# The last batch of an attention and top-k MLP kernel chosen by ranking candidates above a floor, and score columns moved ahead of TensorE's transposes

## The chip, the cores and the metric

The kernel runs on one core of a Trainium2 chip. The metric is the device time of one execution in microseconds. Engines are named as in the profile: PE is TensorE (PEld its weight loads), DVE VectorE, ACT ScalarE, POOL GpSimd, and SP the engine whose queue issues most DMAs.

## The reference, cut to what matters

```python
# q: (4, 12288, 128)   kv: (4, 384, 32, 128)   w_sr: (128, 128)
kv_flat = pool_4x4_mean(kv).reshape(B, 768, 128) @ w_sr
k = v = kv_flat
s = (q @ k.transpose(0, 2, 1)) / sqrt(128)
a = exp(s - s.max(-1)); a /= a.sum(-1) + 1e-9
x = a @ v                                        # (4, 12288, 128)
scores = x @ w_gate                              # (4, 12288)
out = x.copy()
for b in range(4):
    top = argpartition(-scores[b], 128)[:128]    # capacity 128
    ye = relu(x[b, top] @ w1) @ w2               # 128 -> 1024 -> 128
    out[b, top] = x[b, top] + sigmoid(scores[b, top])[:, None] * ye
```

Each batch has 12,288 queries against 768 pooled keys. Of the 12,288 results the 128 with the highest gate score go through a two-layer MLP, and its gated result is added to their rows.

## The kernel before

The queries go in 192 blocks of 256 (48 a batch), each as two halves of 128 (`QT = 2`). A block's scores are a 128 x 1536 tile in PSUM: columns 0 to 767 for the first half, 768 to 1535 for the second. There are two such tiles, `s_buf[0]` and `s_buf[1]`, each three banks wide, and blocks take them in turn. A third tile, `o_two`, of two banks, takes the results of the attention matmuls.

`S(n, parts)` issues the scores of block n in four parts: 0 is columns 0 to 511, 1 is 512 to 767, 2 is 768 to 1023, 3 is 1024 to 1535. Each part is three matmuls, because queries and keys are split into a high piece (`qh`, `kh`) and low pieces (`ql`, `kl`, `kb`). `s_max` takes the row maxima on DVE (`m`), `exp` the exponentials on ACT (`am`), again in parts. In batches 0 to 2 (`by_pe`) PE transposes columns 1280 to 1535 of the exponentials (`turn_pe`), and DMA transposes the rest; in batch 3 DMA transposes all of them. `to_high` casts to 16 bits on ACT, `to_low` takes the remainder on DVE (the last 256 columns) or on POOL (the first 1280), and `turn` issues the DMA transposes on SP's queue (`at`). `AV` multiplies with the values, `LAG = 4` blocks later: 36 matmuls a block. `sums`, `recip` and `finish` normalise on DVE and store through SP. The gate score of each query is one more column of the values; POOL copies it into `scores` for every second block.

The main loop (lines 627 to 681) writes each engine's order out by hand: every engine runs its instructions in the order of the text (`InOrder`). Around the change it reads

```python
        if more:
            S(i + 1, (3,), bank0 + bank1)
        exp(i, 2 if by_pe(i) else 1)
        if by_pe(i):
            turn_pe(i)
        exp(i, 1 if by_pe(i) else 2)
        if more:
            S(i + 1, (2, 1), bank0)
            S(i + 1, (0,))
        to_high(i, 1)
```

Other work is fed in between by generators that stop at named points (`at_point`): the keys of the next batch (`next_keys`), and the top-k and expert of the batch before (`topk`, `pick`, in the list `select`).

After the loop four blocks n-3 to n are still without their attention matmuls (`out`, `norm`, `put`), and batch 2's expert is half done. Block n-3 goes to `o_two`, the other three each to a bank of `s_buf[0]` (`spare`); batch 2's expert writes bank 1 of `o_two`. Then comes the search of batch 3: the scores' bits become sortable 16-bit halves, and `find` determines the 128th largest bit by bit, two bits a step, in eight steps for the high half and eight for the low one. A step is three counting comparisons on DVE, a matmul with ones that sums them over the partitions, and three or four small instructions. Batch 2's remaining pieces advance by one at each step. `pick` turns the mask into the rows' indices with small matmuls against a triangle of ones, gathers the 128 rows by indirect DMA on POOL's queue, while 36 `warm` matmuls keep PE busy, runs the two layers and scatters the result back.

Of the kernel before, what the change touches and what calls it, by code (L numbers as in the profile page):

```python
# [19 lines left out]
P = 128  # L20
# [8 lines left out]
QT = 2  # L29
# [37 lines left out]
def attention_topk_mlp(ctx, tc, a, outs, capacity):  # L67
# [284 lines left out]
    def by_pe(n):  # L352
        return blocks[n][0] < B - 1
# [273 lines left out]
    for i in range(nb):  # L627
# [29 lines left out]
        if more:  # L657
            S(i + 1, (3,), bank0 + bank1)
        exp(i, 2 if by_pe(i) else 1)
# [3 lines left out]
        if more:  # L663
            S(i + 1, (2, 1), bank0)
            S(i + 1, (0,))
# [23 lines left out]
    def out(m):  # L689
        for j in range(QT):  # L690
            AV(m, j, dest[m])
# [15 lines left out]
    key = tk.tile([P, NCOL], I32, name="key")  # L707
    high, low, eqh, rest = (tk.tile([P, NCOL], U16, name=x) for x in ("high", "low", "eqh", "rest16"))
    junk = tk.tile([P, 3, NCOL], BF16, name="junk16")
    jt = tk.tile([P, 3], F32, name="jt")  # L710
    for j in range(3):
        pool.memset(jt[:, j:j + 1], float(j + 1))

    for m in (n - 3, n - 2):
        out(m)
        norm(m)
        put(m)
    out(n - 1)
    out(n)
    key_part(0, NCOL - 2 * QT)  # L720
# [5 lines left out]
    key_part(NCOL - 2 * QT, NCOL)  # L726
    dve.tensor_copy(low, key.bitcast(U16).rearrange("p (n h) -> p n h", h=2)[:, :, 0])

    counts = s_buf[1][:, 0, 0:4]

    def find(x, need, name):
        tv = tk.tile([P, 3], F32, name="tv")
        lo = tk.tile([P, 1], F32, name=name)
        dve.memset(lo, 0.0)
        dve.tensor_scalar(out=tv, in0=jt, scalar1=float(1 << 14), scalar2=None, op0=ALU.mult)
        for sh in range(14, -1, -2):
            cnt = tk.tile([P, 3], BF16, name="cnt3")
            for j in range(3):
                dve.tensor_scalar(out=junk[:, j], in0=x, scalar1=tv[:, j:j + 1], scalar2=None, op0=ALU.is_ge, op1=ALU.add, accum_out=cnt[:, j:j + 1])
            pe.matmul(counts[:, 0:3], ones16, cnt, start=True, stop=True)  # L740
            advance(select)
            if sh:
                base3 = tk.tile([P, 3], F32, name="base3")
                dve.tensor_scalar(out=base3, in0=jt, scalar1=float(1 << (sh - 2)), scalar2=lo, op0=ALU.mult, op1=ALU.add)
            dig = tk.tile([P, 1], F32, name="dig")
            hit = tk.tile([P, 3], F32, name="hit")
            dve.tensor_scalar(out=hit, in0=counts[:, 0:3], scalar1=need, scalar2=None, op0=ALU.is_ge, op1=ALU.add, accum_out=dig)
            if sh:
                tv = tk.tile([P, 3], F32, name="tv")
                dve.scalar_tensor_tensor(out=tv, in0=dig.broadcast_to([P, 3]), scalar=float(1 << sh), in1=base3, op0=ALU.mult, op1=ALU.add)  # L750
            dve.scalar_tensor_tensor(out=lo, in0=dig, scalar=float(1 << sh), in1=lo, op0=ALU.mult, op1=ALU.add)
        return lo

    th = find(high, float(capacity), "th2")
    gth = tk.tile([P, NCOL], BF16, name="gth")
    above = tk.tile([P, 1], BF16, name="above")
    dve.tensor_scalar(out=gth, in0=high, scalar1=th, scalar2=None, op0=ALU.is_gt, op1=ALU.add, accum_out=above)
    dve.tensor_scalar(out=eqh, in0=high, scalar1=th, scalar2=None, op0=ALU.is_equal)
    pe.matmul(counts[:, 3:4], ones16, above, start=True, stop=True)
# [7 lines left out]
    while select:  # L767
        advance(select)
    for _ in pick(b, mask):
        pass  # L770
# [31 lines left out]
```

## Time and profile before

| | us |
|---|---|
| runs | 978.61, 980.33, 980.29 |
| median | 980.29 |
| profiled execution: its time | 976.78 |
| its span, first to last instruction | 975.0 |
| PE busy in the span | 895.4 |
| DVE, ACT, POOL busy | 707.3, 756.1, 749.5 |

The profile is of one execution; times within it are counted from its first instruction. A row of the timeline has the start, the duration, the engine, the operation and what it writes and reads, and in brackets how long the engine stood idle ahead of it and what ended that. Matmuls are pipelined and their ends are modelled, so rows of one engine can overlap.

### The profile page before, as it was taken

Reading aid. Unit: us, or ns where it says so; the run is one execution under the profiler, and the core shown is the slowest. Engines: PE = TensorE matmul, PEld = TensorE weight load, DVE = VectorE, ACT = ScalarE, POOL = GpSimd, SP = SyncE. Lnnn points to the kernel's source line nnn. Section 1 sums busy time; section 2 is a strip of 40 time slices with the busy share of each in tenths; the row PEclk is TensorE's granted clock in tenths of the full one; section 3 lists DMA queues with packets and bytes.
Section 4 is the critical chain, followed back from the end, with each engine's and each line's share of the span. In section 5 each row is a group of like instructions: output and inputs, shape, how many; then the busy total and the mean of one; then the engine's idle time right before and its main releaser. Section 6 shows DMA issues by size and latency. Waiting matters only on the chain.

```text
span 975.0 us, 25800 instructions
## 1 busy us (share of the span) xinstructions
PE 895.4 (92%) x9886; PEld 727.3 (75%) x10067; DVE 707.3 (73%) x1732; ACT 756.1 (78%) x1177; POOL 749.5 (77%) x573
## 2 busy tenths in 40 slices
PE   3889999999999999999999999999999998999844
PEld 2668788777778787787788877787788876887743
DVE  6456666666777777777767777787868876888674
ACT  2668888888888887887888888888798987998700
POOL 1478898887788988888789898988778877688600
PEclk9999999999999999999999999999999999999966
DMA  9799999999999999999999999999999999999910
GB/s 357 207 225 200 246 237 212 219 250 232 223 188 232 232 237 233 228 223 233 212 195 231 234 226 241 221 185 221 180 194 232 240 226 235 253 217 234 224 48 6
DMA packets 600508, 211.31 MB, mean 217 GB/s; under 512 B 532288, under 2 KB 582592, under 8 KB 599616
## 3 DMA queue, kind: packets, MB, share of 16 engines
q1 hardware_dynamic: 600128, 209.12, 104.8%
q8 instruction: 79, 1.29, 0.6%
q0 software_dynamic: 256, 0.52, 0.2%
q14 instruction: 45, 0.37, 0.1%
HBM read 52.04 MB, written 25.43 MB: 79 GB/s over the span
## 4 chain that ended last, share of the span: by engine, by line
PE 62%; DMA 8%; ACT 7%; DVE 7%; issue 6%; POOL 3%; SPq 1%; POOLq 0%; ACTq 0%; DVEq 0%
PE s L52 33%; PE o_two L52 29%; DMA at<-hl 8%; ACT am L52 4%; DVE m L52 3%; ACT hl L52 2%; DVE junk L52 1%; POOL hl L52 1%; POOL ql L52 1%; POOL kv_sum L52 1%; SPq L398 1%; ACT s L52 1%; DVE hit L52 0%; DMA xe<-out,idx 0%; DVE tv L52 0%
## 5 line engine op out<-in xcount | busy, mean ns | idle before, releaser
L52 POOL TENSOR_TENSOR hl<-am,hl 128x1280 bf16<-128x1280 f32 x192 | 503.7, 2624 | 149.4 <-ACT hl L52 69.3
L52 PEld LDWEIGHTS <-at 128*128 128x128 f16 (+1 forms) x6912 | 415.0, 97 | 67.4 <-DMA at<-hl 19.5
L52 PE MATMUL o_two<-vx,at 128*128 128x130 f16 x6804 | 433.1, 220 | 14.4 <-DMA at<-hl 4.9
L52 ACT ACTIVATE am<-s,m 128x512 f32<-128x512 f32 (+1 forms) x528 | 358.4, 707 | 89.6 <-DVE m L52 48.4
L52 DVE TENSOR_REDUCE m<-s 128x2 f32<-128x1536 f32 x192 | 337.2, 1756 | 78.8 <-PE s L52 75.4
L52 PE MATMUL s<-kh,qh 128*128 128x512 f32 (+1 forms) x768 | 286.1, 424 | 1.9 <-POOL ql L52 1.1
L52 ACT CAST hl<-am 128x1280 f16<-128x1280 f32 x192 | 241.6, 1259 | 6.1
L52 PE MATMUL s<-kb,ql 128*128 128x512 bf16 (+1 forms) x697 | 213.8, 322 | 6.3 <-issue 0.2
L52 PE MATMUL s<-kl,qh 128*128 128x256 bf16 (+1 forms) x658 | 203.8, 325 | 0.0
L52 PEld LDWEIGHTS s<-kh,qh 128*128 128x128 f32 x768 | 131.7, 191 | 27.6 <-DVE mg L52 1.1
L52 POOL TENSOR_TENSOR ql<-q_raw,qh 128x512 bf16<-128x512 f32 x96 | 122.4, 1275 | 6.9 <-ACT qh L52 6.9
L52 PEld LDWEIGHTS <-qh 128*128 128x128 bf16 x768 | 75.2, 98 | 47.2 <-issue 39.2
L52 DVE TENSOR_TENSOR at<-s,at 128x256 bf16<-128x256 f32 x144 | 61.1, 425 | 64.7 <-ACT at L52 61.0
L52 DVE TENSOR_TENSOR x<-o_two,rz 128x260 f32<-128x260 f32 x189 | 81.0, 429 | 10.0
L52 ACT CAST at<-s 128x256 f16<-128x256 f32 x144 | 53.6, 372 | 40.9 <-PE s L52 40.9
L52 PEld LDWEIGHTS <-ql 128*128 128x128 bf16 x768 | 76.2, 99 | 4.4 <-POOL ql L52 1.7
L52 DVE TENSOR_SCALAR rz<-o_two,sg 128x2 f32<-128x2 f32 x189 | 41.0, 217 | 39.9 <-PE o_two L52 39.4
L52 PE MATMUL s<-cst,am 128*128 128x128 f32 x288 | 61.1, 294 | 8.7 <-ACT am L52 8.3
L52 PEld LDWEIGHTS s<-cst,am 128*128 128x128 f32 x288 | 31.3, 140 | 49.5 <-ACT am L52 46.1
L52 ACT CAST qh<-q_raw 128x512 fp32r<-128x512 f32 x96 | 58.9, 613 | 1.1 <-DMA q_raw<-in_q 1.1
L52 POOL TENSOR_TENSOR kv_sum<-kv_raw 128x256 f32<-128x256 f32 x72 | 52.2, 726 | 0.0
L52 PEld LDWEIGHTS <-ones 128*128 128x128 bf16 (+1 forms) x291 | 24.5, 108 | 17.6 <-issue 13.4
(163 smaller groups left out, 534.4 us busy)
## 6 DMA issues: line engine op xcount, KB each, us to landing
out<-x SPq DMA_DIRECT2D x96, 256.0 KB, 3.7
q_raw<-in_q SPq DMA_DIRECT2D x93, 256.0 KB, 4.0
kv_raw<-in_kv SPq DMA_DIRECT2D x36, 512.0 KB, 5.4
kv_raw<-in_kv SPq DMA_DIRECT2D x6, 1024.0 KB, 7.6
at<-hl SPq DMA_TRANSPOSE x384, 3.8
w<-in_w SPq DMA_DIRECT2D x2, 512.0 KB, 8.6
q_raw<-in_q SPq DMA_DIRECT2D x1, 768.0 KB
cst<-in_cst SPq DMA_DIRECT2D x1, 320.0 KB, 9.6
```

What stands on the lines that cost most here:

```text
L52: r = f(*args, **kwargs)
L398: nc.sync.dma_start_transpose(out=st[n]["at"][:, h, 0:k // P], in_=st[n]["hl"][:, h, 0:k])
```

## The change

First, in the main loop, part 2 of the next block's scores is issued ahead of the transposes instead of behind them:

```diff
         if more:
             S(i + 1, (3,), bank0 + bank1)
+            S(i + 1, (2,), bank0)
         exp(i, 2 if by_pe(i) else 1)
         if by_pe(i):
             turn_pe(i)
         exp(i, 1 if by_pe(i) else 2)
         if more:
-            S(i + 1, (2, 1), bank0)
+            S(i + 1, (1,), bank0)
             S(i + 1, (0,))
```

Second, the last batch is selected in another way. `floor` takes the two largest scores of each partition among the 88 columns known once block n-4 is finished, ranks these 256 and returns the 128th largest. `choose` takes every score at or above it as a candidate, up to 256 in two slots of 128, runs the expert for both slots, ranks the candidates by their recomputed gate scores, and sets the gate of those behind rank 128 to zero. If there are more than 256 candidates, every gate is zero, and the search as it was (`general`, its steps unchanged) runs behind a branch on a value that all engines read. Scratch space comes from the buffers of the raw keys. The order of the tail changes too: batch 2's remaining pieces go between the blocks' attention matmuls (`drain`).

```diff
-    for m in (n - 3, n - 2):
-        out(m)
-        norm(m)
-        put(m)
-    out(n - 1)
-    out(n)
-    key_part(0, NCOL - 2 * QT)
+    out(n - 3)
+    norm(n - 3)
+    put(n - 3)
+    drain(2)
+    line = floor() if quick else None
+    out(n - 2)
+    norm(n - 2)
+    put(n - 2)
+    drain(2)
+    out(n - 1)
+    drain(2)
+    out(n)
+    while select:
+        advance(select)
     for m in (n - 1, n):
         norm(m)
         lo = blocks[m][1] * QT
         dve.tensor_tensor(out=sc[:, lo:lo + QT], in0=st[m]["o"][:, :, C + 1], in1=st[m]["rz"], op=ALU.mult)
         put(m)
-    key_part(NCOL - 2 * QT, NCOL)
-    dve.tensor_copy(low, key.bitcast(U16).rearrange("p (n h) -> p n h", h=2)[:, :, 0])
...
-    th = find(high, float(capacity), "th2")
...
-    tl = find(rest, need, "tl2")
...
-    for _ in pick(b, mask):
-        pass
+    if quick:
+        over = choose(line)
+        InOrder.last.clear()
+        with tc.If(nc.values_load(over[0:1, 0:1], min_val=0, max_val=1)):
+            general()
+    else:
+        general()
```

The two new functions (allocations of scratch left out):

```python
    def floor():
        dve.max(out=top, in_=sc[:, 0:KNOWN])
        ps = s_flat[(n + 1) % 2][:, 0:1024].rearrange("p (k x) -> p k x", k=2)[:, :, 3 * P:4 * P]
        for s in range(2):
            pe.transpose(ps[:, s], top[:, s:s + 1].broadcast_to([P, P]), ident)
        for s in range(2):
            dve.tensor_scalar(out=junk, in0=ps, scalar1=top[:, s:s + 1], scalar2=None, op0=ALU.is_gt, op1=ALU.add, accum_out=rank[:, s:s + 1])
        dve.tensor_scalar(out=rank, in0=rank, scalar1=float(capacity), scalar2=1e38, op0=ALU.is_ge, op1=ALU.mult)
        dve.tensor_tensor(out=lot, in0=top[:, 0:2], in1=rank, op=ALU.add)
        dve.tensor_tensor(out=low, in0=lot[:, 0:1], in1=lot[:, 1:2], op=ALU.min)
        pe.transpose(ps[:, 0], low.broadcast_to([P, P]), ident)
        dve.tensor_reduce(out=line, in_=ps[:, 0], axis=AX.X, op=ALU.min)
        return line

    def choose(line):
        W = SLOTS * P                                  # SLOTS = 2
        for s in range(SLOTS):
            pool.tensor_scalar(out=jr[:, s * P:(s + 1) * P], in0=jrow, scalar1=float(s * P), scalar2=None, op0=ALU.add)
            pool.tensor_scalar(out=jc[:, s:s + 1], in0=jcol, scalar1=float(s * P), scalar2=None, op0=ALU.add)
        dve.tensor_scalar(out=mask, in0=sc, scalar1=line, scalar2=None, op0=ALU.is_ge, op1=ALU.add, accum_out=mine)
        pe.matmul(inc_ps, mask, tri16, start=True, stop=True)
        pe.matmul(cnt_ps, ones16, mine, start=True, stop=True)
        dve.tensor_copy(inc[0:NCOL], inc_ps)
        dve.tensor_scalar(out=top[:, 0:1], in0=cnt_ps, scalar1=-1.0, scalar2=None, op0=ALU.add)
        pe.matmul(e_ps, tri16[0:NCOL, 0:NCOL], inc[0:NCOL, P - 1:P], start=True, stop=True)
        dve.tensor_scalar(out=over, in0=cnt_ps, scalar1=float(W), scalar2=None, op0=ALU.is_gt)
        dve.tensor_scalar(out=top[:, 1:2], in0=cnt_ps, scalar1=float(W), scalar2=4.0 * W, op0=ALU.is_gt, op1=ALU.mult)
        dve.tensor_scalar(out=jm, in0=jr, scalar1=top[:, 0:1], scalar2=None, op0=ALU.min)
...
        for s in range(SLOTS):
            o = oh[0:NCOL, s * P:(s + 1) * P]
            pe.matmul(g_ps[:, s], o, inc[0:NCOL], start=True, stop=True)
...
        warm(36, near[:, 0:P])
        for s in range(SLOTS):
...
            pool.indirect_dma_start(out=xe[:, s], out_offset=None, in_=outs[b],
                                    in_offset=bass.IndirectOffsetOnAxis(ap=idx[:, s:s + 1], axis=0))
...
        for s in range(SLOTS):
            pe.transpose(x_ps[:, s * P:(s + 1) * P], xe[:, s], ident)
            dve.tensor_copy(xt[:, s * P:(s + 1) * P], x_ps[:, s * P:(s + 1) * P])
            for k in range(2):
                for f in range(FT // 2):
                    pe.matmul(h_ps[2 * s + k][:, f * P:(f + 1) * P], w1[:, (k * FT // 2 + f) * P:(k * FT // 2 + f + 1) * P], xt[:, s * P:(s + 1) * P], start=True, stop=True)
                act.activation(hs[2 * s + k], h_ps[2 * s + k].rearrange("p (f x) -> p f x", x=P), AF.Relu)
            dve.scalar_tensor_tensor(out=gw, in0=xe[:, s], scalar=1.0, in1=wg, op0=ALU.mult, op1=ALU.mult, accum_out=g[:, s:s + 1])
        dve.tensor_tensor(out=gm, in0=g, in1=none, op=ALU.add)
        for s in range(SLOTS):
            pe.transpose(row_ps[:, s * P:(s + 1) * P], gm[:, s:s + 1].broadcast_to([P, P]), ident)
        for s in range(SLOTS):
            for f in range(FT):
                pe.matmul(y_ps[:, s], hs[2 * s + f // (FT // 2)][:, f % (FT // 2)], w2[:, f], start=(f == 0), stop=(f == FT - 1))
...
        for s in range(SLOTS):
            dve.tensor_scalar(out=junk, in0=row_ps, scalar1=g[:, s:s + 1], scalar2=None, op0=ALU.is_gt, op1=ALU.add, accum_out=rank[:, s:s + 1])
            dve.scalar_tensor_tensor(out=junk, in0=row_ps, scalar=g[:, s:s + 1], in1=later[:, s], op0=ALU.is_equal, op1=ALU.mult, accum_out=same[:, s:s + 1])
...
        dve.scalar_tensor_tensor(out=gm, in0=rank, scalar=float(capacity), in1=gm, op0=ALU.is_lt, op1=ALU.mult)
        for s in range(SLOTS):
            dve.scalar_tensor_tensor(out=xo[:, s], in0=y_ps[:, s], scalar=gm[:, s:s + 1], in1=xe[:, s], op0=ALU.mult, op1=ALU.add)
            pool.indirect_dma_start(out=outs[b], out_offset=bass.IndirectOffsetOnAxis(ap=idx[:, s:s + 1], axis=0),
                                    in_=xo[:, s], in_offset=None)
        return over
```

## Rows read from the trace of the kernel before

**Rows 1.** Windows of two batches: length, busy us of each engine, clock, DMA, GB/s.
```profile
258.00:482.00 224.00, 216.08 (x2420) 174.45 (x2466) 173.44 (x410) 186.03 (x291) 193.09 (x150) 1.00 1.13 224
...
708.00:915.00 207.00, 198.95 (x2301) 164.31 (x2337) 161.92 (x383) 182.87 (x274) 159.01 (x101) 0.99 1.16 228
```

**Rows 2.** Timeline, VectorE, clean blocks of batch 0: start us, us, idle before.
```profile
82.75 1.76 DVE L52 TENSOR_REDUCE m<-s 128x2 f32<-128x1536 f32 x1 [0.55 <-PE s L52]
...
87.20 1.76 DVE L52 TENSOR_REDUCE m<-s 128x2 f32<-128x1536 f32 x1 [0.55 <-PE s L52]
```

**Rows 3.** Timeline, TensorE weight loads of the same blocks.
```profile
76.05 0.19 PEld L52 LDWEIGHTS s<-kh,qh 128*128 128x128 f32 x1
...
76.83 0.10 PEld L52 LDWEIGHTS <-qh 128*128 128x128 bf16 x1
...
84.83 0.19 PEld L52 LDWEIGHTS s<-kh,qh 128*128 128x128 f32 x1
85.34 0.20 PEld L52 LDWEIGHTS s<-cst,am 128*128 128x128 f32 x2 [0.33 <-ACT am L52]
...
85.74 0.10 PEld L52 LDWEIGHTS <-qh 128*128 128x128 bf16 x1
```

**Rows 4.** Waits of the weight loads, batches 0 to 2: us, times, longest.
```profile
PEld s L52 <- ACT am L52: 48.0, 115, 2.0
```

**Rows 5.** Timeline, VectorE, clean blocks of batch 3.
```profile
872.61 1.76 DVE L52 TENSOR_REDUCE m<-s 128x2 f32<-128x1536 f32 x1 [0.17 <-PE s L52]
...
876.72 1.76 DVE L52 TENSOR_REDUCE m<-s 128x2 f32<-128x1536 f32 x1 [0.17 <-PE s L52]
```

**Rows 6.** Timeline of the tail, all engines, up to the search.
```profile
915.67 0.28 PE L52 MATMUL s<-cst,xe 128*128 128x128 f32 x1
...
920.67 0.43 DVE L52 TENSOR_TENSOR x<-o_two,rz 128x260 f32<-128x260 f32 x1
...
924.43 2.36 PE L52 MATMUL s<-vx,at 128*128 128x130 f16 x36 [0.98 <-DVE x L52]
...
928.83 1.55 PE L52 MATMUL s<-vx,at 128*128 128x130 f16 x24 [0.59 <-DMA at<-hl]
930.42 0.22 DVE L52 TENSOR_SCALAR rz<-s,sg 128x2 f32<-128x2 f32 x1 [5.02 <-PE s L52]
...
932.14 0.16 DVE L52 TENSOR_SCALAR key<-sc 128x4 int32<-128x4 int32 x1
```

**Rows 7.** Timeline of the search and the selection, all engines.
```profile
933.83 1.14 PE L52 MATMUL o_two<-xt,w 128*128 128x128 f32 x8
...
946.14 0.45 POOL L52 TENSOR_TENSOR xo<-xo,xe 128x128 f32<-128x128 f32 x1 [21.51 <-ACT xo L52]
...
958.07 0.32 DVE L52 SCALAR_TENSOR_TENSOR mask<-rest,tl,gth 128x96 bf16<-128x96 uint16 x1
...
961.99 0.35 DVE L52 TENSOR_SCALAR_CACHE_REDUCE ge<-o_two,rj 128x128 f32<-128x128 f32 x1
...
962.38 0.16 DVE L52 SCALAR_TENSOR_TENSOR idx<-pj,o_two 128x1 uint32<-128x1 f32 x1
```

**Rows 8.** Timeline of the last expert, all engines.
```profile
965.45 0.45 PE L52 MATMUL o_two<-cst,xe 128*128 128x128 f32 x1
...
966.28 2.05 PE L52 MATMUL s<-xt,w 128*128 128x128 f32 x16 [0.39 <-DVE xt L52]
...
970.32 0.35 DVE L52 SCALAR_TENSOR_TENSOR xo<-o_two,g,xe 128x128 f32<-128x128 f32 x1 [0.99 <-PE o_two L52]
970.94 1.00 POOL L52 DMA_INDIRECT out<-xo,idx  x1 [7.16 <-DVE xo L52]
```

**Rows 9.** Windows of the search and of what follows it.
```profile
932.00:958.00 26.00, 9.65 (x49) 7.79 (x49) 22.78 (x188) 1.56 (x3) 1.47 (x2) 0.56 0.04 13
958.00:975.00 17.00, 9.59 (x79) 8.53 (x79) 5.66 (x25) 0.20 (x1) 1.98 (x2) 0.70 0.03 9
```

**Rows 10.** Page, DMA queues: packets, MB, share of 16 engines.
```profile
q8 instruction: 79, 1.29, 0.6%
```

More of the change, by code (lines that the diff above doesn't have):

```diff
@@ L706, in attention_topk_mlp @@
     sc = scores[b]
[L707 to L712, printed above, removed]
-    for m in (n - 3, n - 2):
-        out(m)
-        norm(m)
-        put(m)
+    SLOTS = 2
+    quick = capacity <= P
+    KNOWN = (blocks[n][1] + 1) * QT - 4 * QT
@@ new lines, in attention_topk_mlp, with scratch @@
+    works = [kvp.tile([P, 2, P // 2, TAPS], F32, name="kv_raw").rearrange("p a k t -> p (a k t)") for _ in range(3)]
+    used = [0] * 3
+    def scratch(shape, dt=F32):
+        w = 1
+        for x in shape:
+            w *= x
+        n32 = w if dt in (F32, I32, U32) else (w + 1) // 2
+        i = next(i for i in range(3) if used[i] + n32 <= CHUNK)
+        t = works[i][:, used[i]:used[i] + n32]
+        used[i] += n32
+        if dt != F32:
+            t = t.bitcast(dt)[:, 0:w]
+        if len(shape) == 2:
+            t = t.rearrange("p (a b) -> p a b", a=shape[0])
+        return t
@@ new lines, in floor @@
+    def floor():
+        top = scratch((8,))
+        dve.max(out=top, in_=sc[:, 0:KNOWN])
+        ps = s_flat[(n + 1) % 2][:, 0:1024].rearrange("p (k x) -> p k x", k=2)[:, :, 3 * P:4 * P]
+        for s in range(2):
+            pe.transpose(ps[:, s], top[:, s:s + 1].broadcast_to([P, P]), ident)
+        rank, lot, low = scratch((2,)), scratch((2,)), scratch((1,))
+        junk = scratch((2, P))
+        for s in range(2):
+            dve.tensor_scalar(out=junk, in0=ps, scalar1=top[:, s:s + 1], scalar2=None, op0=ALU.is_gt, op1=ALU.add, accum_out=rank[:, s:s + 1])
[3 more added lines that the diff above has]
+        pe.transpose(ps[:, 0], low.broadcast_to([P, P]), ident)
+        line = scratch((1,))
+        dve.tensor_reduce(out=line, in_=ps[:, 0], axis=AX.X, op=ALU.min)
+        return line
@@ L718, in attention_topk_mlp, with drain @@
+    def drain(k):
+        for _ in range(k):
+            advance(select)
[8 more added lines that the diff above has]
+    drain(2)
     out(n - 1)
+    drain(2)
     out(n)
-    key_part(0, NCOL - 2 * QT)
+    while select:
+        advance(select)
     for m in (n - 1, n):
@@ L725, in attention_topk_mlp @@
         put(m)
-    key_part(NCOL - 2 * QT, NCOL)
-    dve.tensor_copy(low, key.bitcast(U16).rearrange("p (n h) -> p n h", h=2)[:, :, 0])
[L729 to L752, printed above, removed]
@@ L754, in attention_topk_mlp @@
-    th = find(high, float(capacity), "th2")
[L755 to L759, printed above, removed]
-    dve.tensor_tensor(out=rest, in0=low, in1=eqh, op=ALU.mult)
-    need = tk.tile([P, 1], F32, name="need")
```

100 lines of the change are left out of this document (94 added, 6 removed).

## The prediction

> **What bounds the kernel now.** I read the stage windows first, then one attention block engine by engine, then the tail. In the windows TensorE (PE) is busy for 216.08 of 224 us in a middle batch, ScalarE (ACT) 186.03, GpSimd (POOL) 193.09, VectorE (DVE) 173.44 [rows 1], so PE looks like the bound. The block's own rhythm says otherwise. Successive row maxima `m` start 4.45 us apart, each behind an idle 0.55 us that a score matmul ends [rows 2]. The weight load of the transposes stands idle 0.33 us for ACT's `am` in such a block [rows 3]. So the loop is: scores done, maximum, exponential, transposes, and only behind them two thirds of the next block's scores, because PE takes them in order. The view of waits counts 115 such waits, 48.0 us in all [rows 4]. Batch 3, which has no PE transposes, runs a clean block in 4.11 us [rows 5].
>
> The tail is a plain chain. The last attention matmuls end at 928.83 + 1.55 = 930.38, the normalisations start at 930.42 and the search at 932.14 [rows 6]; the mask that ends the search starts at 958.07, the gather's index at 962.38 [rows 7]; the expert runs from 965.45, the scatter is issued at 970.94 [rows 8], and the span ends at 975.0. The search holds 25.9 us of it, VectorE's alone: in that window PE is busy 9.65 of 26 us, ACT 1.56, POOL 1.47 [rows 9].
>
> **Edit 1, score columns 768 to 1023 ahead of the transposes.** Nothing is added; three matmuls change place. From the load of the kh weights for columns 1024 up to the next kl load is 0.78 us where the transposes did not wait (76.05 to 76.83) and 0.91 us where they did (84.83 to 85.74) [rows 3]. The wait therefore costs PE 0.13 us in a clean block, less than the 0.33 shown, since the earlier matmul is still streaming under part of it. The moved matmuls, three of 256 columns, now cover it. At the rate of that 0.78 us, which carries matmuls of 512 and 256 columns and two transposes of 128, they last 0.78 x 768 / 1024 = 0.58; I take 0.3 as cover, since loads and transposes make that stretch dear. The clean period becomes what PE needs, 4.45 - 0.13 = 4.32. As a check from another side, 4.11 plus two transposes, bounded by two of 0.28 [rows 6], lies between 4.11 and 4.67. 115 waits times 0.13 is 15 us [rows 4]. The 48.0 us hold 48.0 - 115 x 0.33 = 10 us beyond the clean wait, in blocks where ACT was late; most of those exceed 0.13 too, up to the 0.3 us of cover. Upper bound 15 + 8 = 23 us.
>
> What is late next: the transposes end some 0.15 us later against the exponential, and ACT's cast of them, ACT's last exponential and cast, and POOL's subtraction queue behind. The cover is the idle time of those engines, by the same windows 38 us of ACT and 31 of POOL per 224 [rows 1], or 0.6 to 0.8 us a block. At 4.32 POOL is at 89%. Where a block with key work takes POOL over its share, the DMA transposes and so the attention matmuls four blocks later wait, and the gain is given back. Lower bound: a loss of 2 us. Clean blocks are the rule, so I take 14 us, near the clean 15.
>
> **Edit 2, the tail before the mask.** In PE's order batch 2's expert pieces and the floor now stand ahead of the attention matmuls of blocks n-2 to n. Batch 2's first four matmuls (1.14 us, rows of 8 [rows 7]) write the bank that block n-3's normalisation reads until 920.67 + 0.43 = 921.10 [rows 6]. They end near 922.3. The floor follows: two transposes (0.28 each [rows 6]) to 922.8, two counting instructions (0.35 [rows 7]), three tiny ones (0.16 each, as the one at 932.14 [rows 6]), a third transpose and a reduction like a count, to about 924.7. DVE's `max` before them has no row; it lies between nothing and 0.35 and is covered by the expert's matmuls. Then 2.36 + 1.14 + 2.36 + 1.14 + 2.36 (n-2, expert, n-1, two result pieces, n) puts the last attention matmul at 934.1, 3.7 us later than 930.38 [rows 6]. It cannot go below 930.38, where block n's transposes land anyway, and if each of the four DVE-to-PE hand-overs costs 0.3 more it is 935.3. Norms and stores take 930.42 to 932.14 [rows 6], unchanged, so the mask starts at 935.9 instead of 958.07. This is 22.2 us won.
>
> **From the mask to the first index.** Before it takes 958.07 to 962.38 + 0.16, 4.5 us [rows 7]. Now one mask matmul and one count replace two, flags and a clamp are added (three of 0.16 and one 256 wide, at most 0.35), and the comparisons are 256 wide for one set instead of 128 wide for two. POOL is the new wait: batch 2's addition (0.45 [rows 7]) and scatter (1.00 [rows 8]) must follow the result pieces, which end at 934.1 + 1.14, and the ramps `jr` queue behind them, two of at most 0.45. They are ready near 938.6, when DVE has wanted the clamp for 0.7 us. I take 5.7 us: index at 941.6. Bounds 4.5 and 7.5. The second slot's index is three DVE instructions later and its gather one POOL slot of 1.00 later, both under the first slot's expert work.
>
> **Two experts instead of one.** Index to transpose takes 965.45 - 962.54 = 2.9 us [rows 7, 8], so the transpose starts at 944.5. To the first matmul 0.83, then 2.05 for a first layer; again 0.8 and 2.05 for the second slot; two row transposes 0.5; two second layers 4.1 (a first layer's 2.05 has the same sixteen instructions) [rows 8]. The output starts at 954.8 instead of 970.32. From there the scatter issue is 0.62 later and the end 4.06 behind that [rows 8]; the second scatter adds 1.0. Span end without the branch: 954.8 + 0.6 + 1.0 + 4.1 = 960.5. The expert's extra 6.4 us is paid in full, since DVE's ranking (four 256-wide counts) hides under the second layers.
>
> **The branch.** No row shows one. All five engines read the flag, compare and jump over the old search. It costs nothing if this lies wholly under the scatter's landing, which is inside the 4.06. Above: the page's instruction queue shows 79 packets at 0.6% of 16 engines, 0.006 x 16 x 975 / 79 = 1.2 us each [rows 10]; two such fetches in a row and the scatter's whole tail of 4.06 again, before the jump instead of beside it, is 6.5. I take 3.0, nearer the fetches, since the end of a program is a point where engines wait for one another already.
>
> The Trainium skill, in "Runtime: NRT & Kernel Launch", section "Instruction fetch mechanics", says that a taken branch out of the current two-page window stalls the engine until the target page is fetched. By that rule one fetch lies on the path; by the row's 1.2 us the sum would be 1.8 us better than with my 3.0, and with five engines fetching one behind another 3 us worse. No run shown so far has such a jump.
>
> **Sum** against the profiled execution (span 975.0, time 976.8): 975.0 - 960.5 = 14.5 won in the tail, 3.0 lost to the branch, 14 won by edit 1, together 25.5: span 949.5, time 951.3. The median of the runs shown is 980.3, 3.5 above the profiled one; the same 25.5 off it gives **955**.
>
> **Rivals.** (a) Edit 1 is given back: POOL or the DMA transposes become what a block waits for. For it: POOL's 89%; against it: batch 3 sustains 4.11 us blocks with 228 GB/s against 224 [rows 1, 5], though without key work on POOL. Time 980.3 - 11.5 = 969. (b) The branch costs its bound or some more, because every DMA must land before it and the engines meet twice: 8 us, time 960. It has no row for or against. (c) PE's clock: in the search stage the granted clock is 0.56 and in the last stage 0.70 [rows 9], that is, it fell to 1.2 GHz while PE was mostly idle. The new chain has PE nearly idle from 935.3 to the index. If the warming matmuls end too early and the two experts run at the lower level, each of their four 2.05 us pieces may double: 8 us, time 963. Against it: the same 36 warming matmuls precede the expert, as before. (d) On the other side: more than 256 scores reach the floor, and the old search runs behind the branch. The floor is the 128th largest of the two best per partition of 88 of 96 columns, so at least 128 pass; an even spread over partitions gives about 160. Only scores crowded in a few partitions reach 257, and from that point it decides: 975.0 - 932.1 = 43 us more, time 998, slower.
>
> **How the numbers follow.** The forecast has 0.60, (a) 0.20, (b) 0.10, (c) 0.05, (d) 0.05. The forecast's own range is 948 to 962: edit 1 from 23 to 8 us, the tail's bounds for half of the rest. To leave no more than 2 in 10 out the range is 945 to 969: it takes in (a), (b), (c) and leaves (d) and the corners where two bounds meet. Faster by over 0.2% (2 us, about what a measurement can tell from no change) has 0.93: the forecast and (a) to (c), less 0.02 within it for the corner where all three meet; slower 0.05, which is (d).
>
> **What would show it.** Right: row maxima 4.3 us apart in clean blocks of batches 0 to 2, and the weight load of the transposes no longer idle for ACT; the last attention matmul some 4 us later against the loop's end; no `find`; two gathers 1 us apart; the 40 us from the last attention matmul to the expert's output turned to 21. Wrong: blocks still at 4.45 (then another edge of the loop binds), more waits of PE for the DMA transposes, more than 6 us between the last scatter's issue and the end, a granted clock of 0.5 in the two experts, or the old search's comparisons in the trace.

## The result, and the profile after

The changed kernel takes 970.42 us (median of 11 executions, 964.55 to 978.01) against 980.33 of the kernel before (11, 974.62 to 984.41): ratio 0.9916 with a 95% interval of 0.989 to 0.9941, so 0.6 to 1.1% faster. Forecast were 955 us and 25.5 us won; 8 to 10 came, and 970.42 lies 1.4 us outside the range. In the two profiled executions the span went from 975.0 to 968.6, 6.4 us. The prediction's terms are compared with these two, and where an experiment says something else than one execution, the experiment decides.

**The loop.** The first fence is VectorE's timeline of the changed kernel, clean blocks of batch 0 (start, us, idle before, releaser):

```profile
83.55 1.76 DVE L52 TENSOR_REDUCE m<-s 128x2 f32<-128x1536 f32 x1 [0.19 <-PE s L52]
87.87 1.76 DVE L52 TENSOR_REDUCE m<-s 128x2 f32<-128x1536 f32 x1 [0.19 <-PE s L52]
```

Row maxima are 4.32 us apart where they were 4.45 [rows 2], as worked out. Not every block is clean: of the 141 intervals between row maxima inside batches 0 to 2, 88 are under 4.50 us in the kernel before and 77 in the changed kernel, there with a median of 4.31, 4.33 and 4.35 in the three batches. The waits of the weight loads over batches 0 to 2 (total us, times, longest), first of the changed kernel:

```profile
PEld s L52 <- ACT am L52: 15.3, 27, 1.9
PEld L52 <- DMA at<-hl: 13.8, 21, 2.1
PEld L52 <- POOL ql L52: 5.3, 12, 1.3
```

then two of the same stretch of the kernel before (the third is [rows 4]):

```profile
PEld L52 <- DMA at<-hl: 8.9, 18, 1.4
...
PEld L52 <- POOL ql L52: 0.9, 1, 0.9
```

The wait for the exponential fell from 48.0 us and 115 times [rows 4] to 15.3 and 27. The waits for the DMA transposes and for the low pieces of the queries grew. The loop's last row maximum shows what was left in these two executions; before, then after:

```profile
914.84 1.76 DVE L52 TENSOR_REDUCE m<-s 128x2 f32<-128x1536 f32 x1
```

```profile
912.90 1.76 DVE L52 TENSOR_REDUCE m<-s 128x2 f32<-128x1536 f32 x1
```

That is 1.9 us of 14.

**The tail.** The timeline of the changed kernel, all engines; to compare with rows of before, add the 1.94 us by which the loop ended earlier:

```profile
930.70 2.22 PE L52 MATMUL s<-vx,at 128*128 128x130 f16 x36
...
934.68 0.30 DVE L52 TENSOR_SCALAR_CACHE_REDUCE kv_raw<-sc,kv_raw 128x96 bf16<-128x96 f32 x1
...
935.05 0.26 PE L52 MATMUL s<-tri,kv_raw 128*96 128x128 bf16 x1 [1.18 <-DVE kv_raw L52]
...
937.42 0.35 DVE L52 TENSOR_SCALAR kv_raw<-kv_raw 128x256 f32<-128x256 f32 x1 [1.24 <-POOL kv_raw L52]
...
938.86 0.48 PE L52 MATMUL s<-kv_raw 96*128 96x128 bf16 x6 [2.94 <-DVE kv_raw L52]
...
939.19 4.00 PE L52 MATMUL s<-ones 128*128 128x128 bf16 x36
...
939.96 0.22 DVE L52 SCALAR_TENSOR_TENSOR kv_raw<-kv_raw,s 128x1 uint32<-128x1 f32 x2
...
943.08 0.45 PE L52 MATMUL s<-cst,kv_raw 128*128 128x128 f32 x1
...
943.90 2.08 PE L52 MATMUL o_two<-kv_raw,w 128*128 128x128 f32 x8 [0.38 <-DVE kv_raw L52]
...
946.02 0.60 ACT L52 ACTIVATE kv_raw<-o_two 128x512 f32<-128x512 f32 x1 [7.77 <-PE o_two L52]
...
946.67 2.07 PE L52 MATMUL o_two<-kv_raw,w 128*128 128x128 f32 x8 [0.69 <-ACT kv_raw L52]
...
952.10 2.07 PE L52 MATMUL s<-kv_raw,w 128*128 128x128 f32 x8 [0.69 <-ACT kv_raw L52]
...
954.86 5.46 PE L52 MATMUL s<-w,kv_raw 128*128 128x128 f32 x32 [0.26 <-ACT kv_raw L52]
...
960.36 0.61 DVE L52 SCALAR_TENSOR_TENSOR kv_raw<-s,kv_raw 128x128 f32<-128x128 f32 x2 [2.83 <-PE s L52]
...
960.99 1.01 POOL L52 DMA_INDIRECT out<-kv_raw  x1 [18.26 <-DVE kv_raw L52]
964.18 0.98 POOL L52 DMA_INDIRECT out<-kv_raw  x1 [2.18 <-DVEq L916]
```

Scratch lies in the raw keys' buffers, so most names read `kv_raw`; the shapes tell the steps apart. The search is gone: the mask starts at 934.68, 936.62 with the shift, where it stood at 958.07 [rows 7]. But eight instructions of a first layer take 2.08 us where sixteen took 2.05 [rows 8], TensorE twice waits 0.69 us for ScalarE, and the second scatter starts 3.19 us behind the first. The window from 940 on (columns as in [rows 1]) has TensorE's granted clock at 0.62 on average, near its lower level of 0.5, which is 1.2 GHz of 2.4:

```profile
940.00:968.00 28.00, 17.93 (x98) 15.93 (x96) 5.92 (x30) 2.48 (x5) 4.03 (x4) 0.62 0.04 11
```

The second scatter's row names VectorE's queue as its releaser, but the chain of waits at the end (start, us, what) has the first scatter's landing between the two scatters:

```profile
960.99 2.39 DMA out<-kv_raw
```

Step by step, in the profiled pair:

| step | forecast | measured | off |
|---|---|---|---|
| edit 1, shift of the loop's end | 14 | 1.94 | 12.1 late |
| mask starts, on the clock of before | 935.9 | 936.62 | 0.7 late |
| mask to first index written | 5.7 | 5.43 | 0.3 early |
| index to transposed input | 2.9 | 2.97 | 0.1 late |
| transposed input to output | 10.3 | 17.28 | 7.0 late |
| output to second scatter's issue | 1.6 | 3.82 | 2.2 late |
| second scatter's issue to the span's end, branch included | 7.1 | 4.46 | 2.6 early |

The index is written at 940.11, the end of the first of the two instructions in the row at 939.96, and the span ends at 968.64. Together 19.1 us late: of the 25.5 forecast, 6.4 are left in this pair.

### The profile page after: what moved, and what is told of

Same layout as the page of the kernel before. It is cut to its first block, busy times and chain, and to the rows that moved or that the text cites. A ratio compares the mean times of both kernels' runs of the same rounds, so it can differ in the third digit from the quotient of the medians.

```text
span 968.6 us, 25898 instructions
## 1 busy us (share of the span) xinstructions
PE 900.3 (93%) x10087; PEld 735.8 (76%) x10087; DVE 686.6 (71%) x1574; ACT 754.7 (78%) x1183; POOL 753.5 (78%) x576
## 4 chain that ended last, share of the span: by engine, by line
PE 56%; DMA 12%; ACT 9%; issue 7%; POOL 5%; DVE 5%; SPq 0%; POOLq 0%; DVEq 0%; ACTq 0%
PE s L52 31%; PE o_two L52 25%; DMA at<-hl 11%; ACT am L52 5%; ACT hl L52 2%; DVE m L52 2%; POOL kv_sum L52 2%; POOL ql L52 1%; POOL hl L52 1%; DMA xe<-out,idx 1%; ACT qh L52 1%; ACT s L52 1%; DVE kv_raw L52 0%; POOL out L52 0%; SPq L398 0%
## 5 line engine op out<-in xcount | busy, mean ns | idle before, releaser
L52 PE MATMUL s<-kh,qh 128*128 128x512 f32 (+1 forms) x768 | 251.9, 409 | 1.5 <-DVE mg L52 1.5
L52 PE MATMUL s<-kl,qh 128*128 128x512 bf16 (+1 forms) x768 | 253.1, 333 | 0.0
L52 PE MATMUL s<-kb,ql 128*128 128x512 bf16 (+1 forms) x768 | 248.8, 327 | 2.5 <-POOL ql L52 2.0
L52 PE MATMUL s<-cst,am 128*128 128x128 f32 x288 | 56.7, 279 | 6.4 <-ACT am L52 6.0
L52 PEld LDWEIGHTS s<-cst,am 128*128 128x128 f32 x288 | 34.8, 142 | 14.9 <-ACT am L52 13.4
L52 DVE RECIPROCAL rz<-rz 128x2 f32<-128x2 f32 x192 | 31.9, 166 | 6.6
```

Of the source, the lines that this page charges most:

```text
L52: r = f(*args, **kwargs)
```

## The experiments

Single profiles of one loop differ: in five kernels whose loop has the same text (the changed one and the four tail runs below) it ends between 912.77 and 918.45 us, and the loop of the kernel before ends at 914.84 there and at 921.56 in `e2_tail_only`, with the same text. So effects in the loop are read from medians and ratios, and small ones in the tail from the steps of the profile. Each ratio is to the kernel before on the same chip, and its brackets hold the 95% interval.

**The two edits apart.** `e1_order_only` is the kernel before with edit 1 alone; `e2_tail_only` is the changed kernel with edit 1 undone.

> The kernel before with edit 1 alone (score columns 768 to 1023 ahead of the transposes). My prediction said 14 us won (ratio 0.986). Theory Q (given back: clean blocks fall to 4.32 us, but GpSimd's queue, and with it the low parts and the DMA transposes, falls behind in the blocks with key work or a query split): 0 to 4 us won, ratio 0.996 to 1.0, and more waits of TensorE for the DMA transposes and for the low query part than before. Theory T (the loss is in the tail alone and edit 1 pays in full): 10 us or more.

> The changed kernel with edit 1 undone (order of the scores as before). Theory Q: it keeps nearly all of the measured gain, 5 to 8 us against before (ratio 0.992 to 0.995), with clean blocks back at 4.45 us. If edit 1 pays in full, it is 10 us or more slower than the changed kernel, ratio over 1.0.

Edit 1 alone: 977.59 against 979.43, ratio 0.999 (0.9967 to 1.0012). The tail alone: 970.88, ratio 0.9907 (0.9875 to 0.994). So, as far as these intervals tell, the whole measured gain is the tail's: 9.1 us by its ratio, where the prediction had 11.5 for tail and branch, and 1.0 us for edit 1, where it had 14. The waits of the weight loads with edit 1 alone, over batches 0 to 2:

```profile
PEld L52 <- DMA at<-hl: 18.8, 30, 2.0
PEld L52 <- POOL ql L52: 5.0, 11, 1.3
```

Against the kernel before, the waits for DMA transposes grew by 9.9 us and those for POOL's `ql` by 4.1. A weight load can stand idle while matmuls run, so this is more than TensorE lost. The matmuls' own waits for the transposes over the same stretch, before and with edit 1 alone:

```profile
PE o_two L52 <- DMA at<-hl: 3.7, 7, 1.2
```

```profile
PE o_two L52 <- DMA at<-hl: 10.9, 17, 1.5
```

They grew by 7.2 us, and those for `ql` from 0.6 to 2.8. Seven profiles whose loop has edit 1 and loads of 512 KB (this one, the changed kernel and the tail runs `t1` to `t5` below) have 13.8 to 18.8 us of weight loads waiting for transposes, the two in the old order 8.9 and 10.2: the growth is clear, its size is not. Which of the two waits is the cause, the next runs ask.

**Is it POOL's queue?** Two pairs take work off POOL, each without and with edit 1. The first moves the subtraction that makes `ql` to VectorE:

```diff
-        pool.tensor_tensor(out=ql, in0=raw, in1=qh.bitcast(F32), op=ALU.subtract)
+        dve.tensor_tensor(out=ql, in0=raw, in1=qh.bitcast(F32), op=ALU.subtract)
```

> The kernel before with the subtraction that makes the low query part (512 wide, one in two blocks, 1.27 us) on VectorE instead of GpSimd; same results. It takes 0.64 us a block from GpSimd and gives VectorE at most that. Theory Q (GpSimd's queue sets the blocks that are not clean): 2 to 8 us won, the loop still holding clean blocks at 4.45. Rival D (the DMA transposes themselves, or the queue that issues them, are at their limit): same as before within 2 us.

> The same with edit 1 as well. Theory Q: with GpSimd relieved edit 1 pays, 8 to 15 us more than without it (ratio to before 0.975 to 0.985). Rival D: edit 1 adds no more here than it does in e1, 0 to 4 us.

1118.62 (ratio 1.1408) and 1137.54 (1.1606), a miss. The page's group of that subtraction in `e3_ql_dve`, busy us and mean ns of one:

```profile
L52 DVE TENSOR_TENSOR ql<-q_raw,qh 128x512 bf16<-128x512 f32 x96 | 237.1, 2470 | 16.2 <-ACT qh L52 15.9
```

In the kernel before POOL does it in 1275 ns:

```profile
L52 POOL TENSOR_TENSOR ql<-q_raw,qh 128x512 bf16<-128x512 f32 x96 | 122.4, 1275 | 6.9 <-ACT qh L52 6.9
```

The expectation had VectorE lose at most 0.64 us a block. The 2470 ns are mostly waiting. In 94 of the 96 cases VectorE's `ql` begins while POOL's subtraction `hl` runs, and it ends 0.54 to 0.56 us behind it; in the two others POOL is idle and it takes 0.69 and 0.68 us. One of the 94 and one of the two:

```profile
97.01 2.62 POOL L52 TENSOR_TENSOR hl<-am,hl 128x1280 bf16<-128x1280 f32 x1 [2.00 <-issue]
97.46 2.71 DVE L52 TENSOR_TENSOR ql<-q_raw,qh 128x512 bf16<-128x512 f32 x1
```

```profile
31.92 0.68 DVE L52 TENSOR_TENSOR ql<-q_raw,qh 128x512 bf16<-128x512 f32 x1
```

VectorE is in the loop from row maximum to exponential, so holding it for 2470 ns in every second block makes a new bound, and the pair tells nothing of the theories. The second pair leaves most of the key additions out:

```diff
-                pool.tensor_tensor(out=o, in0=x, in1=y, op=ALU.add)
+                if h == 6:
+                    pool.tensor_tensor(out=pooled, in0=t[:, :, 0], in1=t[:, :, 1], op=ALU.add)
```

> The kernel before with six of the seven GpSimd additions per key tile left out in batches 1 to 3 (each key is then made of 2 of its 16 taps); the key loads and all else stay. GpSimd has 3.9 us less to do in seven blocks. Theory Q (GpSimd's queue): 2 to 6 us won. Theory D (DMA transposes late for their queue or for DMA bandwidth): 0 to 2 us.

> The same with edit 1. Theory Q: 8 us or more faster than without it. Theory D: no more than edit 1 gives by itself, 0 to 4 us faster than without it, with TensorE's waits for the DMA transposes as in edit 1 alone.

973.64 (0.9951, 0.9927 to 0.9975) and 973.11 (0.9943, 0.9921 to 0.9965). The relief by itself wins 4.8 us by the ratio, inside theory Q's 2 to 6: POOL's queue does cost the kernel before something. But with POOL busy some 75 us less over batches 0 to 2, edit 1 still brings only 0.5 us where theory Q asked 8. Its weight loads, with edit 1:

```profile
PEld L52 <- DMA at<-hl: 11.1, 12, 2.2
PEld L52 <- POOL ql L52: 0.7, 1, 0.7
```

POOL's wait is gone, the transposes' is not. As the reason why edit 1 does not pay, POOL's queue falls.

**Is it the DMA engines' load?** The key loads of batches 1 to 3 are left out; the additions run on the expert's weights instead, so POOL's work stays and the later batches' keys are not the reference's:

```diff
-            if kc + 1 < KT:
-                raws[kc + 1] = load_kv(b, kc + 1, -2)
-            t = raws[kc]
...
+            t = w1.rearrange("p (k t) -> p k t", t=TAPS)
```

> The kernel before with the key loads of batches 1 to 3 left out (their additions run in full, on the first layer's weights in place of the keys, so keys of those batches are wrong). 18 MB of some 210 MB are not moved and their issues leave SP's queue. Theory D: 3 to 8 us won, fewer waits of TensorE for the transposes. Theory Q: same within 2 us.

> The same with edit 1. Theory D: edit 1 now pays, 8 us or more faster than without it. Theory Q: 0 to 4 us, as in edit 1 alone.

971.33 (0.9934, 0.991 to 0.9957) and 963.13 (0.9831, 0.9805 to 0.9856): here edit 1 brings 8.2 us by the medians and 10.1 by the ratios, clear of the intervals. The weight loads still wait for `ql`:

```profile
PEld L52 <- POOL ql L52: 5.7, 14, 1.3
```

No wait of TensorE for a transpose of the exponentials is left in either run. From its issue to its landing a transpose takes 3.4 us in both (median over batches 0 to 2); in the kernel before it takes 4.0, with edit 1 alone 4.1. So behind its issue a transpose is hardly later with edit 1; the shorter block needs it earlier, and while the keys load it comes too late. That takes most of edit 1's gain in the real kernel. Whether the bytes, their place in the shared queue or their issue from SP make the transposes late, this pair doesn't separate. The rest of the 14 is not won here either.

**Bursts or amount?** The same bytes in quarters of 256 KB at every second addition, instead of halves of 512 KB at every fourth:

```diff
-                raws[kc + 1] = load_kv(b, kc + 1, -2)
+                raws[kc + 1] = load_kv(b, kc + 1, -4)
...
-                if h == 3 and kc + 1 < KT:
-                    load_kv(b, kc + 1, -2, raws[kc + 1])
+                if h in (1, 3, 5) and kc + 1 < KT:
+                    load_kv(b, kc + 1, -4, raws[kc + 1], (h + 1) // 2)
```

> The kernel before with the key loads of batches 1 to 3 in quarters of 256 KB, issued at every second addition, instead of halves of 512 KB at every fourth. Nothing is left out and the bytes are the same. It is the base for the next run. Theory burst: transposes queue behind a large load; smaller pieces cut TensorE's waits for the transposes (3.7 us before) and the time by 1 to 3 us. Theory amount: no change (within 1.5 us).

> The same with the score columns 768 to 1023 ahead of the transposes. Theory burst: the order then pays 5 to 8 us against the run before it, as it paid 8.2 us with the key loads left out, and the median landing of a transpose in batch 2 stays near 3.4 us. Theory amount: as in the changed kernel, the transposes land in 4.3 us, TensorE waits some 8 us for them and the order pays less than 2 us.

976.85 (0.9971, 0.9951 to 0.9991) and 974.08 (0.9943, 0.9918 to 0.9968). The smaller pieces by themselves take 2.8 us off by the ratio, and edit 1 brings another 2.8, between the two theories; its two intervals overlap, so it is not shown to be more than nothing. The weight loads' waits for transposes, without it and with it:

```profile
PEld L52 <- DMA at<-hl: 8.8, 14, 2.0
```

```profile
PEld L52 <- DMA at<-hl: 12.9, 16, 2.5
```

The expectations count the matmuls' own waits, 3.7 us before; these are 5.2 and 7.9 here. So the smaller pieces did not cut the waits in the old order (8.9 to 8.8, 3.7 to 5.2), as theory burst had it. With edit 1 they grow by 4.1 instead of 9.9, but 12.9 is only just below the 13.8 to 18.8 of the seven profiles. The median landing of a transpose in the second batch (258 to 482 us) is 4.4 and 4.2 us in these two, 3.4 before, 4.3 with edit 1 alone and in the changed kernel, and 3.4 in `t5_tail_all`, which has the changed kernel's loop: in one batch of one execution it was a poor gauge.

**The tail's suspects, one by one**, all on the changed kernel. By the ratios these four runs lie between 0.7 us over and 2.2 us under the changed kernel, with intervals that overlap its own, so they are read from the steps of their profiles. First, the halves of a first layer go to two PSUM tiles in turn:

```diff
-        h_ps = [o_two[:, 0], o_two[:, 1], near[:, 0:512], near[:, 512:1024]]
+        h_ps = [o_two[:, 0], near[:, 0:512], o_two[:, 1], near[:, 512:1024]]
```

> The changed kernel, with one difference: the two halves of a slot's first layer write different PSUM tiles (o_two and the free score tile in turn) instead of the two banks of one. Nothing is left out. Theory T: TensorE stood idle 0.69 us ahead of the second half of each slot's first layer because ScalarE's relu of the first half was still reading the same tile. Then both waits are gone, the output is written about 1.4 us earlier after the first expert matmul, and the time is about 1.4 us under the changed kernel's (969 against 970.4). Rival: the wait is for ScalarE's destination or for the clock of the engine; then the two idle times stay and the time does not move.

968.75 (0.9897, 0.986 to 0.9935). Its timeline, second half of the first slot, and both halves of the second:

```profile
949.42 1.91 PE L52 MATMUL s<-kv_raw,w 128*128 128x128 f32 x8
...
952.02 1.13 PE L52 MATMUL o_two<-kv_raw,w 128*128 128x128 f32 x8 [0.48 <-ACT kv_raw L52]
952.99 1.06 PE L52 MATMUL s<-kv_raw,w 128*128 128x128 f32 x8
```

Both 0.69 us waits ahead of a second half are gone, so it was the shared tile. The clock rose during the experts here too (1.13 and 1.06 for eight), so the 11.9 us of its experts are not this edit's alone.

Second, more idle matmuls, so that TensorE doesn't rest ahead of the index:

```diff
+        warm(36, x_ps[:, 0:P])
         pe.matmul(inc_ps, mask, tri16, start=True, stop=True)
...
         pe.matmul(e_ps, tri16[0:NCOL, 0:NCOL], inc[0:NCOL, P - 1:P], start=True, stop=True)
+        warm(40, o_two[:, 0, 0:P])
...
-        warm(36, near[:, 0:P])
+        warm(60, near[:, 0:P])
```

> The changed kernel with more idle matmuls that keep TensorE busy in the last selection: 36 ahead of the mask's matmul, 40 behind the second selection matmul, and 60 instead of 36 behind the one-hot matmuls. Nothing is left out. Theory K: the eight instructions of half a first layer took 2.08 us, where sixteen took 2.05 before, because TensorE had fallen to its lower clock while it waited for the index. With it busy, four halves cost 1.04 us less each and the 32 instructions of the second layers 4.1 instead of 5.46: 4 to 5.5 us off the time (about 965.5), granted clock near 1.0 in the experts' window instead of 0.62. Rival: the pieces are long for another reason, such as the wait for ScalarE between them; then eight instructions still take 2.08 us. Third: the idle matmuls stand in the way of the selection's own and cost up to 3 us.

969.56 (0.9923, 0.9896 to 0.995): by the time it can't be told from the changed kernel, and this profile's loop ended 5.6 us later, at 918.45. The steps show the effect:

```profile
944.83 3.51 PE L52 MATMUL s<-ones 128*128 128x128 bf16 x60
...
949.40 1.16 PE L52 MATMUL o_two<-kv_raw,w 128*128 128x128 f32 x8 [0.43 <-DVE kv_raw L52]
...
951.25 1.16 PE L52 MATMUL o_two<-kv_raw,w 128*128 128x128 f32 x8 [0.69 <-ACT kv_raw L52]
...
956.59 3.84 PE L52 MATMUL s<-w,kv_raw 128*128 128x128 f32 x32 [0.47 <-ACT kv_raw L52]
```

An idle matmul takes 0.059 us here and 0.111 in the changed kernel (4.00 for 36), half a first layer 1.16 instead of 2.08, the second layers 3.84 instead of 5.46. From transposed input to output it is 11.80 us instead of 17.28: the lower clock cost 5.5 in that profile. In the runs `t3_no_branch` and `t4_free_scatter` below, the clock rose in the middle of the experts and the same stretch took 14.72 and 14.73. In `e2_tail_only`, whose tail has the changed kernel's text, the same 36 idle matmuls ran at the lower clock, and yet it was back for the first half layer:

```profile
946.43 4.00 PE L52 MATMUL s<-ones 128*128 128x128 bf16 x36
...
950.33 0.30 PE L52 MATMUL s<-cst,kv_raw 128*128 128x128 f32 x1
...
951.01 1.16 PE L52 MATMUL o_two<-kv_raw,w 128*128 128x128 f32 x8 [0.38 <-DVE kv_raw L52]
...
962.08 0.61 DVE L52 SCALAR_TENSOR_TENSOR kv_raw<-s,kv_raw 128x128 f32<-128x128 f32 x2 [1.42 <-PE s L52]
```

Its stretch takes 11.75 us. So this text lost between nothing and 5.5 us to the clock, from execution to execution. With the idle matmuls of `t2_warm`, or the 18, 40 and 60 of the four runs further down, every half layer ran at the upper level in all five profiles.

Third and fourth, the branch taken out (and with it the general search), and the second scatter freed from the first:

> The changed kernel without the branch and without the general search behind it (left out: the search that would run with more than 256 candidates, which this data does not reach). By the prediction's term the branch costs 3.0 us, so the time would be about 967.4, and the time from the last scatter's issue to the span's end about 3 us shorter than the 4.4 of the changed kernel. By the trace of the changed kernel, where the jump's rows take 0.2 to 1.3 us beside the scatter's landing, it costs 0 to 1.3 us: 969 to 970.4.

> The changed kernel, where the second slot's scatter no longer waits for the first one's landing (the two write different rows of the same output). Nothing is left out. Theory: the 2.18 us between the two scatters is a wait for the first one's landing, so that the second is issued right behind it: the span's end comes 2.2 us earlier, time about 968.2. Rival: the queue of GpSimd or the descriptors of the first scatter hold the second back anyway; then it is issued as late as before and nothing moves.

968.52 (0.9903, 0.987 to 0.9935) and 967.39 (0.9894, 0.9866 to 0.9922). Without the branch the last scatter is at 968.02 of a span of 972.15, so 4.13 us to the end instead of 4.46 (4.45 to 4.51 in all nine profiles with the branch): the branch costs 0.3 us there, and 0.4 from the first scatter on. With the scatter freed its row reads

```profile
961.03 0.98 POOL L52 DMA_INDIRECT out<-kv_raw  x1 [0.30 <-DMA out<-xo,idx]
```

1.32 us behind the first at 959.71, where it was 3.19. That is 1.9 us, and the wait was for the landing.

**All three together, and a version that beats both kernels.** `t5_tail_all` is the changed kernel with two tiles, idle matmuls (18, 40, 60) and the freed scatter; `t6_tail_all_quarters` has the key loads in quarters as well.

> The changed kernel with three differences in the tail: the halves of a first layer in different PSUM tiles, idle matmuls that keep TensorE busy (18, 40 and 60), and the second scatter not waiting for the first. Nothing is left out. If the three account for the shortfall of the tail, the time from the mask's matmul to the end of the span falls from 33.6 us to about 25 (0.7 less to the index, 6.9 less in the experts, 1.8 less behind them), and the time is 8 to 9 us under the changed kernel's, about 962. Rival: with the clock high another wait takes over, the relu of ScalarE or the weights, and the experts' part stays above 12 us: 965 to 967.

> The run before it with the key loads in quarters too. Theory burst: 5 us under it, since the order of the score columns then pays. Theory amount: the same time within 1.5 us.

966.39 (0.9869, 0.9838 to 0.99) and 959.33 (0.9796, 0.9769 to 0.9824). From `t5_tail_all`:

```profile
936.20 0.26 PE L52 MATMUL s<-tri,kv_raw 128*96 128x128 bf16 x1 [0.18 <-DVE kv_raw L52]
...
944.11 0.30 PE L52 MATMUL s<-cst,kv_raw 128*128 128x128 f32 x1 [0.35 <-DMA kv_raw<-out,kv_raw]
...
945.80 1.06 PE L52 MATMUL s<-kv_raw,w 128*128 128x128 f32 x8
...
954.03 0.61 DVE L52 SCALAR_TENSOR_TENSOR kv_raw<-s,kv_raw 128x128 f32<-128x128 f32 x2 [1.42 <-PE s L52]
```

From the mask's matmul to the span's end it takes 960.4 - 936.20 = 24.2 us, against 968.6 - 935.05 = 33.55: the three account for the tail's whole shortfall, and from transposed input to output it is 9.92, where 10.3 were forecast. The loop ended at 912.96, as in the changed kernel's profile, and that pair of executions differs by 8.1 us. The medians differ by 4.0 only, where 8 to 9 were forecast. The changed kernel's profile met the low clock in all four halves, other executions of the same tail text did not, as `e2_tail_only`, `t3_no_branch` and `t4_free_scatter` show; the mean granted clock of its eleven executions is 0.979 to 0.989, of the profiled one 0.982. This would account for part of the difference; how much is not shown. `t6_tail_all_quarters` is the fastest measured, 2.0% under the kernel before and 7.1 us under `t5_tail_all`, where theory burst had 5. Two runs ask what is left of edit 1 in it:

> The fastest version so far (all three tail edits, key loads in quarters; 959.3 us, ratio 0.9796 to the kernel before) with the score columns 768 to 1023 behind the transposes again. Nothing is left out. Theory burst: with small pieces the order pays most of what it paid without key loads, so this run is 5 to 8 us slower, 964 to 967 (ratio 0.985 to 0.988). Theory amount: the order pays under 2 us, 959 to 961 (ratio 0.980 to 0.982).

> The fastest version so far with the key loads in eighths of 128 KB, one at each addition. Nothing is left out, same bytes. Theory burst: TensorE's waits for the transposes (12.4 us of the weight loads in the fastest version, 18.8 with halves) fall again, towards the none of the run without key loads, and the time by 1 to 3 us, to 957. Theory amount: the waits and the time stay (958.5 to 961), or rise as more issues stand in SyncE's queue.

With the old order 963.22 (0.982, 0.9791 to 0.985): edit 1 is worth 2.4 us by the ratios, again between the theories and within the intervals, so the 7.1 us of the quarters are not mostly the order's. With eighths (one 128 KB piece at each addition) 972.06 (0.9927, 0.9903 to 0.9951), 12.7 us slower, and the waits for the transposes are longer still:

```profile
PEld L52 <- DMA at<-hl: 23.9, 30, 3.8
```

So "the smaller the piece, the shorter the wait" is wrong. From issue to landing a transpose takes 3.9 us here, no longer than with halves (4.1; medians over batches 0 to 2), so either its issue is late or a few land very late; the runs don't tell which. Why quarters help and eighths harm stays open: the size of the pieces, their number in SyncE's queue and the times at which they are issued changed together.

## Why the prediction was wrong, point by point

**What bounds the kernel**: right. The loop from scores to exponential to transposes was what a clean block waited for, and the search was the tail's.

**Edit 1**: the clean period was right (4.32 in batch 0), the term was not. The step that failed is "Clean blocks are the rule, so I take 14 us". It failed twice. The 115 waits that were multiplied by 0.13 are not 115 clean blocks: 88 intervals are clean before, and at the 0.14, 0.12 and 0.10 us that they shortened in batches 0, 1 and 2 they are worth some 10 us, an estimate from the two traces that fits the 8.2 to 10.1 of the pair without key loads. And nearly all of that was given back. The prediction's list of cover named the idle time of ACT and POOL and left out the DMA transposes, which it named a sentence later as what gives the gain back. The runs show 8.2 us with the key loads gone, 0.5 with POOL relieved, 1.8 by medians and 1.0 by the ratio in the real kernel. More waits for the transposes stood among the prediction's signs of being wrong. That is rival (a), with chance 0.20, and in it the DMA half; its evidence, POOL's 89%, pointed at the other half. What spoke against (a), batch 3 at 4.11 us and 228 GB/s, had no key loads among its bytes: the rate was no measure of how late a transpose comes.

**The tail up to the transposed input**: right within 0.7 us at each step; the last attention matmul ends 20.0 us behind the loop's last row maximum, 4.5 later than the 15.5 before. VectorE waits 1.24 us for POOL's ramps, where 0.7 was worked out.

**The experts**: the step that failed is two first layers at 2.05 with 0.8 between, and 4.1 for the second layers. The sum itself holds: 9.92 us in `t5_tail_all`. Two things were missed. The clock is rival (c), given 0.05 and 8 us; it cost 5.5 in this profile. The argument against it was that the same 36 idle matmuls run ahead of the expert as before. They ran at the lower level before as well:

```profile
961.62 4.00 PE L52 MATMUL s<-ones 128*128 128x128 bf16 x36
```

There the clock was back for the first layer (sixteen instructions in 2.05 us), in `e2_tail_only` too, and in the changed kernel's profile only during the second layers. So these matmuls did not hold the clock up; that it was back in time before was luck, which the prediction took for their doing. The other 1.9 us (11.80 to 9.92) go with the shared tile, two waits of 0.69 us for ScalarE and the overlap of the halves that they prevent, which no step had: in the old selection the halves went to two score tiles, in the new one each pair shares a tile.

**The second scatter**: sized at its issue of 1.0 us. It waits for the first one's landing, 2.2 us more: both write the same tensor.

**The branch**: 3.0 us were taken without a row, between bounds of 0 and 6.5; its removal brings 0.3 to 0.4 in the profile. The Trainium skill's rule ("Runtime: NRT & Kernel Launch", section "Instruction fetch mechanics"), that a taken branch out of the fetched window stalls for the target page, shows nowhere as a microsecond on this path; a fetch under the scatter's landing would not be seen. Rival (b), 8 us, is out, and so is (d): the trace holds no comparison of the old search.

Of the 19.1 us, 12.1 are a rival that was named and underrated, 5.5 the clock, another such rival, and some 4 a second instance of a step (second half, second scatter) costed as if it were free of the first; the branch, costed too high, gives 2.6 back. This is the profiled pair, whose tail met the low clock; by the medians and ratios the tail's shortfall is smaller, and most of the miss is edit 1.

## What to carry to other kernels

When a change shortens the critical loop, price it against every resource that the loop was slower than, the DMA queues first; here a pair of runs without the loads said in one step what the busy shares did not. When a tail does the same step twice, check what the second instance shares with the first: a PSUM tile, a destination tensor. When a chain of small steps leaves TensorE idle, keep it busy before the clock falls, not after, and read the clock in that window in more than one execution. When an instruction moves between VectorE and POOL, look at what the other engine runs beside it before pricing it.

## What the runs showed of the hardware that was not expected

- A subtraction of 128 x 512 with f32 operands takes 0.69 us on VectorE while POOL is idle; begun during POOL's subtraction of 128 x 1280, it ended 0.54 to 0.56 us behind that one in 94 of 94 cases of `e3_ql_dve`, 2470 ns on average over all 96.
- Idle matmuls that begin at the lower clock bring it back at different times: behind 36 of them (4.00 us) the four halves all ran at half speed in the changed kernel's profile, and none of them in `e2_tail_only`, with the same text.
- A branch that all five engines read and jump by costs 0.3 us beside a scatter's landing.
- With 18 MB of key loads left out, a DMA transpose lands 3.4 us after its issue instead of 4.0 (medians over batches 0 to 2).
- Key loads of 128 KB pieces made a kernel 12.7 us slower than 256 KB pieces of the same bytes.
